# A linear-attention and bilinear feed-forward kernel: fewer and wider unread products, three weight pieces moved forward, one more tile in the planned stage

## The chip, the cores and the metric

The kernel runs on one core of one Trainium2 chip. A core has TensorE (PE in the profile; its weight loads are PEld), VectorE (DVE), ScalarE (ACT), GpSimd (POOL) and SyncE (SP), each with its own queue of instructions that it works off in order. SP mostly issues DMAs; ACT and POOL issue a few too. The metric is the device time of one execution in microseconds (us).

## What is computed

```python
# q, k, v, f_logit: (4, 8, 768, 48) float32
f = 1 / (1 + exp(-f_logit))
for t in range(768):
    state = f[:, :, t, :, None] * state + einsum('bhd,bhe->bhde', k[:, :, t], v[:, :, t])
    y[:, :, t] = einsum('bhd,bhde->bhe', q[:, :, t], state)
x = y.transpose(0, 2, 1, 3).reshape(3072, 384)
# w_a, w_b: (384, 1536), w_out: (1536, 384)
out = ((x @ w_a) * (x @ w_b)) @ w_out
```

The first part is a linear attention with a decay per channel, over 4 batches and 8 heads; the second a bilinear feed-forward block over 3072 tokens. The three weight matrices come as 64-bit floats and are turned into 32-bit ones on the chip, bit by bit[...].

## The kernel before

**Attention** is cut into 16 units: a batch, a half of its 768 positions (384, `BLK`) and four of its eight heads. A unit has fronts and a core. The front (`front_parts`, L296) makes the sigmoids of f on ACT (L306, L309), an affine step on POOL (L312), running products of f and of its inverse by scans on DVE (L316, L329), and multiplies k and q by them (L333). The core takes scores on PE (`scores`, L387), masks them on DVE (`mask`, L400), transposes k (`turn` on PE, L411; `turned`, its copy out on ACT), makes the gains of the state (`gains`, L435) and sums them (`carried`, L462 and L464), and adds the part within a chunk (`within`, L484) and the part that comes from the state (`across`, L510). ACT and DVE copy the result out of PSUM (`out_of_bank`, L529), and DMAs (`stored`, L549) bring it, transposed by its layout, into `xT`, a block of 384 tokens by 384 channels. Two units make a block; there are 8 blocks.

**Weights** come in 20 pieces (`weight_pieces`, L36): pieces 1 and 2 are the first 128 columns of w_b and w_a, then pairs of w_b and w_a for 256 columns each, then 128 columns again, then six pieces of w_out. `load_weights` issues the DMA of the next piece on SP into one of four raw buffers (pieces 5 and 6 have places of their own). `from_double` (L52) converts one in three parts: two ACT passes (L58, L59) and one POOL pass (L60); two more ACT passes (L62, L63); then DVE passes (L68, and L73, one for each of three row groups). `begin(n)` emits the first two parts up to piece n (`begin(8.5)` stops after the first part of piece 9), `end(n)` the third part, and after most pieces one more `load_weights`. A tile of the feed-forward part, `up(blk, ft)`, is 6 calls (12 matmul records, L593) for 128 columns of w_b and of w_a and one block; it needs `needed(ft)` pieces ended: tile 3 needs six, tiles 7 and 8 need ten. `product()` copies the w_b result of the oldest tile on ACT and multiplies it on DVE (L613, L615), which gives its two PSUM banks back; there are four such banks.

**Order.** The head of the kernel, up to the call of `up(0, 5)` and a little beyond (L965 to L1084), is an order written out by hand for all engines: units 0 to 3, the first weight pieces and tiles 0 to 5 of block 0. `keep_up(n)` (L954) emits n products of the identity with itself into a PSUM bank that nobody reads. Then a loop over `ups` (L1092) emits one tile after the other with the conversions between them; its length is `alone`. The remaining tiles of block 1 and everything after them form the list `main`: for blocks 2 to 7 a scheme with fewer multiplications for the first product (`up_triples`, its matmuls at L715), and for all blocks one for the second (`down`, matmuls at L808). A list scheduler (L1132 to L1274) walks through `main`; at every step its `fill` places work of the other lines (fronts, cores, loads, sums of weights, of w_out and of x) where its cost estimates find room by `BEAT`, the time of one call on PE. It knows the engines as free when it starts.

What the change and the steps below touch:

- `keep_up` at L953 to L957, called at L982, L988 and L1031, each time ahead of work that comes from other engines: `turn(0)`, `turn(1)` and `up(0, 0)`
- `end(6)` at L1060, `begin(8.5)` at L1079, `begin(9)` at L1083, with `up(0, 2)` to `up(0, 5)`, `across(3)` and `y_of(3)` (three ACT copies and five SP stores) around them
- `alone` at L1091
- `products_of_f[0]`, the running products of f of unit 0, which lie in `groups`

Of the kernel before, what the change touches and what calls it, by code (L numbers as in the profile page):

```python
# [22 lines left out]
BLK = 384  # L23
# [12 lines left out]
def weight_pieces(w_ba, w_out, moe_w_a, moe_w_b, moe_w_out, apart=1):  # L36


    w_b, w_a = (w_ba[:, i] for i in range(2))
    NKT, NFT, DM = w_ba.shape[2], w_out.shape[1], w_out.shape[2]  # L40
    for ft, n in [(0, 1)] + [(ft, 2) for ft in range(1, NFT - 1, 2)] + [(NFT - 1, 1)]:
        for dst, src in ((w_b, moe_w_b), (w_a, moe_w_a)):
            cols = slice(ft * 128, (ft + n) * 128)
            yield dst[:, :, cols], src.rearrange("(kt p) c -> p kt c", p=128)[:, :, cols], (NKT, n * 128)
    for ft in range(0, NFT, 2):
        rows = moe_w_out[ft * 128:(ft + 2) * 128]
        place = w_out.rearrange("p (j k) c -> p k j c", j=apart)
        to = place[:, ft // apart, ft % apart:ft % apart + 2] if apart > 1 else w_out[:, ft:ft + 2]
        yield to, rows.rearrange("(k p) c -> p k c", p=128), (2, DM)


def from_double(nc, dst, raw, k, h, bit, sgn, whole, apart=False):  # L52

    words = raw.bitcast(U32).rearrange("p k (n two) -> p (k n) two", two=2)
    lo, hi = words[:, :, 0], words[:, :, 1]
    width = lo.shape[1]
    h, bit, sgn = (x[:, 0:width] for x in (h, bit, sgn))
    nc.scalar.activation(h, hi.bitcast(FP32), AF.Abs, scale=HI_SCALE)  # L58
    nc.scalar.activation(bit.bitcast(FP32), lo, AF.Identity, bias=whole, scale=2.0**-29)  # L59
    nc.gpsimd.tensor_scalar(h, h, HI_MAX, None, ALU.min)  # L60
    yield
    nc.scalar.activation(sgn, hi.bitcast(FP32), AF.Sign)  # L62
    nc.scalar.activation(  # L63
        bit.bitcast(U16).rearrange("p (n two) -> p n two", two=2)[:, :, 1], sgn, AF.Relu, scale=-32768.0
    )
    yield
    hu = h.bitcast(U32)
    nc.vector.tensor_scalar(hu, hu, 3, None, ALU.logical_shift_left)  # L68
    hu, bit = (x.rearrange("p (k n) -> p k n", k=k) for x in (hu, bit))
    dst = dst.bitcast(U32)  # L70

    for rows in ([slice(i, i + 1) for i in range(k)] if apart else [slice(0, k)]):
        nc.vector.tensor_tensor(dst[:, rows], hu[:, rows], bit[:, rows], ALU.add)  # L73
    yield
# [62 lines left out]
def by_quotients(ctx, tc, q, k, f_logit, v, moe_w_a, moe_w_b, moe_w_out, out, ident, weights, bad):  # L137
    nc = tc.nc
# [60 lines left out]
    def load_unit(u, names="fkqv"):  # L199
        for do in loads_of(u, names):  # L200
            do()
# [34 lines left out]
    todo, raws, going = list(weight_pieces(w_ba, w_out, moe_w_a, moe_w_b, moe_w_out, NFT // 3)), [], []  # L236
    begun, ended = [0], [0]

    def load_weights(n=1):
        for _ in range(n):  # L240
            if len(raws) == len(todo):
                return
            dst, src, (k, m) = todo[len(raws)]
            raw = dst
            if src.dtype != FP32:

                if len(raws) in EARLY:
                    raw = groups[:, EARLY.index(len(raws))].bitcast(mybir.dt.uint64)
                else:
                    raw = next(raw_places)  # L250
                raw = raw[:, 0:k * m].rearrange("p (k m) -> p k m", k=k)
            nc.sync.dma_start(out=raw, in_=src)
            raws.append(raw)

    def begin(n):

        while 2 * n > begun[0] < 2 * len(todo):
            i, second = divmod(begun[0], 2)
            dst, src, shape = todo[i]
            if not second:  # L260
                going.append(
                    from_double(
                        nc, dst, raws[i], shape[0], next(blocks), bits[i % len(bits)], sign, whole, shape[0] == NKT
                    )
                    if src.dtype != FP32 else iter(())
                )
            next(going[i], None)
            begun[0] += 1

    def end(n):  # L270

        while ended[0] < min(n, len(todo)):
            begin(ended[0] + 1)
            next(going[ended[0]], None)
            ended[0] += 1
            if ended[0] > 2 and ended[0] - 1 not in EARLY:
                load_weights()
# [12 lines left out]
    products_of_f = {u: firsts[:, u] if u in FIRST else sets[u % NSET]["f"] for u in range(NU)}  # L290
# [60 lines left out]
    ps_f = [ps_a.tile([128, 512], FP32, tag=f"ps_f{i}", name=f"ps_f{i}") for i in range(4)]  # L351
    idle = list(range(4))
# [50 lines left out]
    def turn(u):  # L403

        kf = halves(sets[u % NSET]["k"])
        live.setdefault(u, {})["kT"] = sb1.tile([128, 2, NC, 128], FP32, tag="kT", name="kT")
        ps = live[u]["turned"] = [ps_f[idle.pop(0)] for _ in range(2)] if u in FIRST else pair_of(away(u))
        for n in range(2):
            for c in range(NC):
                o = n * BLK + c * C  # L410
                nc.tensor.transpose(ps[n][:, c * C:c * C + C], kf[:, o:o + C], ident)  # L411
# [10 lines left out]
    def gains(u, chunks=range(NC)):  # L422

        _, half, _ = unit(u)
        t, kT = sets[u % NSET], live[u]["kT"]
        last = half == NH - 1
        ps = live[u]["turned"]
        for n in range(2):
            for c in chunks:
                for p in range(2):  # L430
                    if last and c == NC - 1 and p == 1:
                        continue
                    for h in range(2):
                        r = slice(SUB * p, SUB * p + SUB)
                        nc.tensor.matmul(  # L435
                            ps[p][R * h:R * h + D, (n * NC + c) * D:(n * NC + c) * D + D],
                            lhsT=kT[r, n, c, R * h:R * h + D],
                            rhs=t["v"][r, n, c, h * D:h * D + D],
                            start=True,
                            stop=True,  # L440
                        )
        if chunks[0]:
            return
        st = sb3.tile([128, NJ, 2, D], FP32, tag="st", name="st")
        before = live[u - NQ]["st"][NJ] if half else None
        live[u]["st"] = [before] + [st[:, j] for j in range(NJ - 1 if last else NJ)]
# [46 lines left out]
    def across(u):  # L493

        b, half, qd = unit(u)
        qf, st, ps = halves(sets[u % NSET]["q"]), live[u]["st"], live[u]["y"]

        order = [(n, c, o, p) for n, c, o in each() for p in range(2)]
        if u in FIRST:

            order = sorted(order[::-1], key=lambda x: -x[3])
        elif half:
            order = [(n, c, o, p) for n, c, o in reversed(list(each())) for p in range(2)]
        for n, c, o, p in order:
            j = 2 * c + p
            if j == half == 0:
                continue
            for h in range(2):
                r, e = slice(R * h, R * h + D), R * (p ^ h)
                nc.tensor.matmul(  # L510
                    ps[p][e:e + D, o:o + SUB],
                    lhsT=st[j][r, n],
                    rhs=qf[r, tokens(n, c, p)],
                    start=False,
                    stop=True,
                    skip_group_check=True,
                )
# [63 lines left out]
    def up(blk, ft):  # L581

        for _, _, _, do, *args in up_steps(blk, ft):
            do(*args)
# [353 lines left out]
    with tc.manual_schedule():  # L938
# [14 lines left out]

        def keep_up(n):  # L954

            for _ in range(n):
                nc.tensor.matmul(ps_f[idle[-1]][:, 0:128], lhsT=ident, rhs=ident, start=True, stop=True)  # L957

        def y_of(u):
            for part in range(3):  # L960
                out_of_bank(u, part)
            stored(u)
# [16 lines left out]
        for _ in range(3):  # L979
            next(fronts[0])  # L980
        begin(1)
        keep_up(9)  # L982
        turn(0)
        turned(0)
        scores(0)
        begin(2)
        gains(0)
        keep_up(12)  # L988
        for _ in range(3):
            next(fronts[1])  # L990
        turn(1)
# [36 lines left out]
        load_weights()  # L1028
        load_unit(3, "k")
        load_unit(3, "q")  # L1030
        keep_up(30)  # L1031
        up(0, 0)
        emit_all(others[1])
        begin(4)
# [20 lines left out]
        begin(6.5)  # L1055
        up(0, 2)
        across(2)
        end(5)
        next(fronts[3])
        end(6)  # L1060
        y_of(2)
        load_weights(2)
        product()
# [12 lines left out]
        end(8)  # L1076
        carried(3)
        product()
        begin(8.5)  # L1079
        up(0, 5)  # L1080
        across(3)
        y_of(3)
        begin(9)  # L1083
        product()  # L1084


# [1 line left out]
        for i in range(8, NFT):  # L1088
            ups += [(1, i - 8), (0, i)]
        ups += [(1, i) for i in range(NFT - 8, NFT)]  # L1090
        alone = len(todo) - 6  # L1091
        for n, (blk, i) in enumerate(ups[0:alone]):  # L1092
            convert(needed(i))
            up(blk, i)
# [528 lines left out]
```

## Time and profile before

| | |
|---|---|
| three runs | 604.84, 607.16, 608.56 us, median 607.16 |
| the profiled execution | 606.54 us, of which the span of the instructions is 604.70 |
| busy: PE, DVE, ACT, POOL | 577.5, 411.9, 268.7, 76.3 us |
| mean granted TensorE clock | 0.991 |
| largest idle times of PE after the first 30 us | 2.44 (before 76.61), 1.13 (before 56.09), 0.93 (before 260.08), 0.62 (before 85.40), 0.62 (before 146.28) |

By stage, busy time of PE, DVE and ACT in us:

| stretch, us | what runs | PE | DVE | ACT |
|---|---|---|---|---|
| 0 to 34 | units 0 and 1, first weights | 21.42 | 25.46 | 18.70 |
| 34 to 86 | tiles 0 to 7 of block 0, units 2 and 3 | 47.81 | 34.34 | 42.41 |
| 86 to 128 | tiles one by one, weights | 42.00 | 19.57 | 31.13 |
| 128 to 196 | planned: last tiles of block 1, first `down` | 67.32 | 60.47 | 22.09 |
| 196 to 310 | planned: blocks 2 and 3 | 111.08 | 92.14 | 54.79 |
| 310 to 605 | planned: the rest | 287.91 | 179.96 | 99.61 |

A row of the timeline gives the start, the time that a run of like instructions takes, the engine, the line, the operation, what it writes and reads, their number, and in brackets the idle time of that engine before it with what ended that. A call of `matmul` on 32-bit floats shows as two records.

### The profile page before, as it was taken

To read this page: it belongs to the slowest core of one execution; us is meant where nothing else is said; L and a number is where in the kernel's file an instruction comes from. 1 tells how busy PE (TensorE), PEld (TensorE's weight loads), DVE (VectorE), ACT (ScalarE), POOL (GpSimd) and SP (SyncE) were. 2 spreads that over 40 slices of the span, in tenths; PEclk is the share of its full clock that TensorE was granted. 3 is DMA by queue.
4 is the path that set the end of the run, shared out by engine and by line. 5 is a ranking of instruction groups with operands and counts; after the bars stand their busy time and mean duration, and the time that the engine had idled before them with its cause. 6 is when DMAs were issued, how large, how long until landed. Compare 5 with 4: busy or idle time off the path is not lost.

```text
span 604.7 us, 14106 instructions
## 1 busy us (share of the span) xinstructions
PE 577.5 (96%) x5880; PEld 521.3 (86%) x5880; DVE 411.9 (68%) x786; ACT 268.7 (44%) x507; POOL 76.3 (13%) x71
## 2 busy tenths in 40 slices
PE   3899989999999999999999999999999999999995
PEld 3785545556999999989989999999999999999995
DVE  6889344568988768968895768846775165745741
ACT  5578588853321546325531353326331335134300
POOL 6254144435200000000000000000000000000000
PEclk9799999999999999999999999999999999999998
DMA  8685579239945134044003420032001100000000
GB/s 214 174 249 174 193 219 294 68 54 171 174 113 135 37 80 98 4 119 105 2 2 83 114 55 2 1 86 60 2 1 48 47 0 1 2 26 1 1 29 31
DMA packets 33273, 49.44 MB, mean 82 GB/s; under 512 B 3952, under 2 KB 24976, under 8 KB 33200
## 3 DMA queue, kind: packets, MB, share of 16 engines
q1 hardware_dynamic: 30000, 42.38, 25.7%
q0 software_dynamic: 3056, 5.92, 5.7%
q8 instruction: 48, 0.79, 0.6%
q14 instruction: 25, 0.20, 0.1%
q10 hardware_dynamic: 144, 0.15, 0.1%
HBM read 33.23 MB, written 4.72 MB: 63 GB/s over the span
## 4 chain that ended last, share of the span: by engine, by line
PE 80%; DVE 11%; ACT 4%; issue 3%; DMA 1%; SPq 0%; DVEq 0%; ACTq 0%
PE ps_f L715 33%; PE ps_f L808 26%; PE ps_f L593 12%; PE ps_y L484 2%; DVE groups L707 2%; PE ps_x L387 2%; PE ps_y L510 2%; DVE sums L707 1%; DVE inv L329 1%; PE ps_x L435 1%; PE ps_f L957 1%; PE ps_x L411 1%; DVE f_in L316 1%; DVE st L464 1%; DVE spare L329 1%
## 5 line engine op out<-in xcount | busy, mean ns | idle before, releaser
L593 PE MATMUL ps_f<-xT,w_ba 128*128 128x384 f32 x288 | 96.0, 490 | 4.2 <-DVE w_ba L73 3.6
L1271 ACT COPY sums<-ps_f 128x384 f32<-128x384 f32 x120 | 57.5, 480 | 85.1 <-PE ps_f L715 75.7
L593 PEld LDWEIGHTS ps_f<-xT,w_ba 128*128 128x128 f32 x288 | 53.6, 190 | 41.8 <-ACT spare L59 3.0
L1271 ACT COPY groups<-ps_f 128x384 f32<-128x384 f32 x120 | 57.7, 481 | 59.6 <-PE ps_f L715 39.3
L715 PE MATMUL ps_f<-xT,w_ba 128*128 128x192 f32 x384 | 78.2, 326 | 0.0
L715 PEld LDWEIGHTS ps_f<-xT,w_ba 128*128 128x128 f32 x384 | 64.7, 190 | 0.1
L715 PE MATMUL ps_f<-x_sums,raw 128*128 128x192 f32 x288 | 53.7, 330 | 1.9 <-DVE groups L707 1.3
L715 PE MATMUL ps_f<-groups,w_ba 128*128 128x192 f32 x288 | 55.5, 328 | 0.0
L808 PE MATMUL ps_f<-w_out,groups 128*128 128x192 f32 x288 | 51.8, 329 | 0.6 <-ACT x_sums L613 0.6
L808 PE MATMUL ps_f<-w_out,sums 128*128 128x192 f32 x288 | 51.9, 328 | 0.0
L715 PEld LDWEIGHTS ps_f<-x_sums,raw 128*128 128x128 f32 x288 | 47.0, 190 | 5.0 <-DVE groups L707 2.9
L808 PE MATMUL ps_f<-spare,sums 128*128 128x192 f32 x288 | 49.5, 327 | 0.0
L808 PEld LDWEIGHTS ps_f<-w_out,groups 128*128 128x128 f32 x288 | 47.1, 190 | 1.6 <-ACT x_sums L613 1.2
L715 PEld LDWEIGHTS ps_f<-groups,w_ba 128*128 128x128 f32 x288 | 47.9, 190 | 0.4 <-ACT groups L1271 0.2
L808 PEld LDWEIGHTS ps_f<-w_out,sums 128*128 128x128 f32 x288 | 47.2, 190 | 0.4
L808 PEld LDWEIGHTS ps_f<-spare,sums 128*128 128x128 f32 x288 | 47.1, 190 | 0.1
L312 POOL TENSOR_SCALAR inv<-inv 128x768 f32<-128x768 f32 x14 | 13.1, 935 | 267.4 <-ACT inv L309 267.3
L60 POOL TENSOR_SCALAR sums<-sums 128x768 f32<-128x768 f32 (+1 forms) x20 | 39.1, 1954 | 51.7 <-ACT sums L58 47.1
L707 DVE TENSOR_TENSOR sums<-sums,groups 128x768 f32<-128x768 f32 x36 | 34.9, 970 | 14.3 <-ACT groups L1271 13.9
L707 DVE TENSOR_TENSOR sums<-ps_f,sums 128x384 f32<-128x384 f32 x60 | 32.8, 552 | 15.6 <-PE ps_f L715 14.3
L715 PE MATMUL ps_f<-xT,raw 128*128 128x192 f32 x192 | 39.6, 329 | 0.5 <-ACT sums L1271 0.5
L715 PE MATMUL ps_f<-x_sums,w_ba 128*128 128x192 f32 x192 | 39.2, 327 | 0.0
(136 smaller groups left out, 883.4 us busy)
## 6 DMA issues: line engine op xcount, KB each, us to landing
raw<-w_ba POOLq DMA_DIRECT2D x11, 512.0 KB, 7.8
k_in<-in_k_dram SPq DMA_DIRECT2D x32, 144.0 KB, 4.4
q_in<-in_q_dram SPq DMA_DIRECT2D x32, 144.0 KB, 4.7
v_in<-in_v_dram SPq DMA_DIRECT2D x16, 288.0 KB, 5.2
raw<-in_moe_w_out_dram SPq DMA_DIRECT2D x6, 768.0 KB, 5.7
out_dram<-o SPq DMA_DIRECT2D x24, 192.0 KB, 1.9
f_in<-in_f_logit_dram SPq DMA_DIRECT2D x28, 144.0 KB, 3.0
xT<-y SPq DMA_DIRECT2D x45, 72.0 KB, 2.1
```

What stands on the lines that cost most here:

```text
L60: nc.gpsimd.tensor_scalar(h, h, HI_MAX, None, ALU.min)
L312: nc.gpsimd.tensor_scalar(inv, inv, EXP_K, 1.0, ALU.mult, ALU.add)
L316: nc.vector.tensor_tensor_scan(F[:, c], F[:, c], none, math.exp(MIDDLE), ALU.mult, ALU.add)
L329: nc.vector.tensor_tensor_scan(inv[:, w], inv[:, w], none[:, 0:C], first, ALU.mult, ALU.add)
L387: nc.tensor.matmul(ps[h][SUB * p:SUB * p + SUB, o:o + SUB], lhsT=kf[r, tokens(n, c, p)], rhs=qf[r, tokens(n, c, p)], start=True, stop=True,)
L484: nc.tensor.matmul(ps[p][e:e + D, o:o + SUB], lhsT=t["v"][r, n, c, h * D:h * D + D], rhs=at[r, h, o:o + SUB], start=o == 0, stop=True, ski ...
L510: nc.tensor.matmul(ps[p][e:e + D, o:o + SUB], lhsT=st[j][r, n], rhs=qf[r, tokens(n, c, p)], start=False, stop=True, skip_group_check=True,)
L593: nc.tensor.matmul(ps[nm][:, 0:BLK], lhsT=w[:, kt, ft * 128:ft * 128 + 128], rhs=xT[blk][:, kt], start=kt == 0, stop=kt == NKT - 1,)
L707: nc.vector.tensor_tensor(to, x, y, op)
L715: nc.tensor.matmul(ps[:, g], lhsT=sums_of_w[name][:, g, 128 * j:128 * j + 128], rhs=sums_of_x[blk][name], start=start and g == 0, stop=Tru ...
L808: nc.tensor.matmul(to, lhsT=x[:, i // 2, i % 2], rhs=w[:, NI * (i % 2) + i // 2], start=start and i == 0, stop=i == HFT - 1, skip_group_ch ...
L1271: do(*args)
```

## The change

Three things. `keep_up` multiplies the identity with the running products of f of unit 0 instead of with itself, 384 columns wide instead of 128, and is called for 2, 4 and 6 calls instead of 9, 12 and 30. In the order written by hand, the last conversion part of piece 6 stands ahead of the products of k and q of unit 3 (`next(fronts[3])`); and ahead of `up(0, 5)` stand the first two parts of pieces 9 and 10 and the last part of piece 9 (with the load of piece 13 that follows it), where the first part of piece 9 stood there alone, its second part after `y_of(3)`, and the rest in the loop. The loop makes 13 tiles instead of 14, so tile 7 of block 1 comes into the planned list.

```diff
         def keep_up(n):
 
+            x = products_of_f[0][:, 0]
             for _ in range(n):
-                nc.tensor.matmul(ps_f[idle[-1]][:, 0:128], lhsT=ident, rhs=ident, start=True, stop=True)
+                nc.tensor.matmul(ps_f[idle[-1]][:, 0:BLK], lhsT=ident, rhs=x, start=True, stop=True)
...
         begin(1)
-        keep_up(9)
+        keep_up(2)
         turn(0)
         turned(0)
         scores(0)
         begin(2)
         gains(0)
-        keep_up(12)
+        keep_up(4)
...
-        keep_up(30)
+        keep_up(6)
         up(0, 0)
...
         up(0, 2)
         across(2)
-        end(5)
+        end(6)
         next(fronts[3])
-        end(6)
         y_of(2)
...
         carried(3)
         product()
-        begin(8.5)
+        begin(10)
+        end(9)
         up(0, 5)
         across(3)
         y_of(3)
-        begin(9)
         product()
...
-        alone = len(todo) - 6
+        alone = len(todo) - 7
         for n, (blk, i) in enumerate(ups[0:alone]):
             convert(needed(i))
             up(blk, i)
```

## The prediction

> **What bounds the kernel now.** I read the page first, then the chain of waits, then PE's timeline for each idle stretch, and then the other engines there.
>
> ```profile
> PE 577.5 (96%) x5880; PEld 521.3 (86%) x5880; DVE 411.9 (68%) x786; ACT 268.7 (44%) x507; POOL 76.3 (13%) x71
> PE   3899989999999999999999999999999999999995
> PEclk9799999999999999999999999999999999999998
> ```
>
> TensorE is busy 577.5 of 604.7 us, and the chain puts 80% of the span on it. The change takes no arithmetic away from what is computed, so it can win only TensorE's idle time, time on unread products, and time at a reduced clock. Nearly all of that lies before 86 us. PE's timeline, with the idle time before a row in brackets:
>
> ```profile
> 29.61 7.54 PE L957 MATMUL ps_f<-ident 128*128 128x128 f32 x60
> 36.99 4.04 PE L593 MATMUL ps_f<-xT,w_ba 128*128 128x384 f32 x12
> 56.09 2.20 PE L593 MATMUL ps_f<-xT,w_ba 128*128 128x384 f32 x6 [1.13 <-DVE w_ba L73]
> 76.61 8.17 PE L593 MATMUL ps_f<-xT,w_ba 128*128 128x384 f32 x24 [2.44 <-DVE w_ba L73]
> 85.40 55.74 PE L593 MATMUL ps_f<-xT,w_ba 128*128 128x384 f32 x172 [0.62 <-ACT x_sums L613]
> ```
>
> There are four places: unread products right before the first tile of the feed-forward part, and three waits of 1.13, 2.44 and 0.62 us for converted weights or for a bank that an ACT copy empties. From 85.40 on the tiles follow each other without a gap.
>
> **Unread products.** One call is two matmul records. The 30 narrow ones at 29.61 take 7.54 us. A 128x384 record takes 4.04/12 = 0.33 us at full clock, so six wide calls are 12 x 0.33 = 4.0 us. They start at half clock, as now:
>
> ```profile
> 21.00:22.00 1.00, 0.22 (x16) 0.07 (x7) 0.93 (x4) 0.97 (x3) 0.58 (x1) 1.00 1.10 265
> 24.00:24.50 0.50, 0.33 (x12) 0.33 (x16) 0.50 (x4) 0.00 (x0) 0.50 (x1) 0.52 0.06 15
> 30.50:31.00 0.50, 0.50 (x5) 0.50 (x5) 0.47 (x2) 0.00 (x0) 0.00 (x0) 0.65 0.46 129
> 31.00:31.50 0.50, 0.50 (x7) 0.50 (x6) 0.50 (x1) 0.00 (x0) 0.24 (x1) 1.00 0.37 105
> ```
>
> (Columns: stretch, length, busy PE, PEld, DVE, ACT, POOL, granted clock, DMA share, GB/s.) The clock is half from about 24.0 to 30.8. From 29.61 to 30.83 two wide records pass at 0.65 us, the other ten take 3.3: the end is at about 34.2 instead of 37.1. The first tile then waits for its input, which DMAs bring:
>
> ```profile
> xT<-groups ACTq DMA_DIRECT2D x1, 48.0 KB, 3.3
> raw<-in_moe_w_a_dram SPq DMA_DIRECT2D x1, 768.0 KB, 6.7
> ```
>
> (Issue to landing, last column.) The last store of xT on ACT's queue is issued at 32.3 and lands at 35.6; the last of SP at 31.95 + 3.3 = 35.25. So the tile starts at about 35.5 instead of 36.99, 1.5 us sooner, with some 1.3 us of idle PE before it. Of the 3.5 us cut, 2.0 are hidden by the stores.
>
> The other two groups, 9 to 2 and 12 to 4 (1152 to 768 and 1536 to 1536 columns), I cost at nothing: they stand at 10.38 to 14.1 and 16.25 to 19.2, where DVE runs unbroken (scans L316 and L329, products L333) and what follows waits for DVE (transposes for k at 12.6 and 18.9, scores for q at 13.5 and 19.75). If that cover were gone, the sum of their changes is about 1.4 us the first time and 0.3 the second. The products now also wait for the scan whose result they read; it ends at 7.9, before the identity that they wait for anyway (10.38). POOL and SP are not touched there.
>
> *A rule against this.* The rows: PE busy 1.17 us of the 3.0 from 21 to 24 was followed by half clock, but the gap of 2.44 us before 76.61 was not (granted clock 1.00 in every 2 us there). The Trainium skill, "TensorE: Matmul & The Clock Gate", Part 1, says that a free-running window of about 3.4 us decides: a busy one opens the clock, an idle one halves it[...]. By the rule a gap of 1.3 us leaves the clock alone and costs 0; by the row of 21 to 24 a window 39% busy is enough for half clock, and a window with 1.3 us idle is 62% busy, so it lies nearer to the gap at 74 that did no harm. If it did, one window at half clock costs 3.4/2 = 1.7 us and eats the 1.5. For the first group the rule asks for 3.4 us of work; two wide calls at half clock are 4 x 0.65 = 2.6 us, then transposes. If the clock stays half one window longer, cold scores (1.5 instead of 0.9 us) and gains push the second transpose by some 0.7 us, hidden; two windows longer push it from 19 to 22.3 and mask(1) by 2 us. The other way, a clock that is not halved at 24 saves about 2 us of the small products until 29.6. I take 0, bounds -2 and +2.
>
> **Sixth piece.** Its DVE half stands behind two products of k and q:
>
> ```profile
> 53.19 0.95 DVE L333 TENSOR_TENSOR k_in<-k_in,spare 128x768 f32<-128x768 f32 x1
> 54.06 0.95 DVE L333 TENSOR_TENSOR q_in<-q_in,f_in 128x768 f32<-128x768 f32 x1
> 54.92 0.55 DVE L68 TENSOR_SCALAR sums<-sums 128x768 uint32<-128x768 uint32 x1
> ```
>
> Its ACT half ended at 50.05. Put ahead of them, its first row is ready 1.75 us sooner, at about 54.3, and tile (0,3) goes from its first to its second half at 54.96 without the wait of 1.13. The two products come 1.7 us later (k at 55.8, q at 56.7), but the transposes that need them follow the tile at 57.1: still covered. No DMA is issued by this step. The DVE chain before it also starts sooner: mask(2) waits 0.99 us for scores(2) at 42.63, and with the tile 1.5 us sooner DVE reaches it at 41.64, 1.0 us gained. PE on its own is then at tile (0,3) at 51.55 and DVE's first row of piece five at 51.5: together 58.29 becomes 55.65, **2.6 us** for these two edits.
>
> **Ninth and tenth piece.** ACT is the bound from 70 to 86:
>
> ```profile
> 63.17 1.00 ACT L59 ACTIVATE spare<-raw,whole 128x768 f32<-128x768 uint32 x1
> 70.19 1.46 ACT L529 COPY y<-ps_y 128x384 f32<-128x384 f32 x3 [6.02 <-PE ps_y L510]
> 71.68 0.90 ACT L62 ACTIVATE spare<-raw 128x768 bf16<-128x768 f32 x1
> 73.54 0.83 ACT L613 COPY x_sums<-ps_f 128x384 f32<-128x384 f32 x2
> 84.90 0.82 ACT L613 COPY x_sums<-ps_f 128x384 f32<-128x384 f32 x2
> ```
>
> ACT idles 6.02 us because y_of(3) waits for across(3), and then has everything to do at once. The change puts the second half of piece nine (0.90 + 1.06) and all of piece ten (3.6) into that hole: 5.6 us into 6.0. POOL's 2.2 us for piece ten moves with it (POOL is idle 9.74 us there), DVE's 2.2 us for piece nine fall into DVE's idle 6.88. On SP the load of piece thirteen (0.38 us) now stands ahead of the five stores of y_of(3); it waits for the raw buffer of piece nine, free about 65, long before the first store. Piece ten's load, issued at 57.64, lands 6.7 us later, at 64.3, just when ACT gets to it. Moved to the new times: pieces nine and ten on ACT 61.1 to 68.3, y_of(3) to 69.8 (PE's across(3) ends at 67.5), two copies, pieces eleven and twelve 70.7 to 77.8, the bank of tile (0,7) free at 78.8, needed at 79.6. Tile (0,7) finds its weights at 71.6, block 1's input lands at 74.2 and is needed at 75.7. So both waits go: **2.44 + 0.62 = 3.1 us**. If y_of(3) slips by more than 0.8 us, the bank is late and part of the 0.62 comes back.
>
> **One tile more in the list.** Planned work may start 3.9 us (one tile) sooner, before 128, where DVE is less than half busy:
>
> ```profile
> 128.00:196.00 68.00, 67.32 (x775) 58.55 (x774) 60.47 (x121) 22.09 (x39) 16.66 (x15) 1.00 0.74 142
> 196.00:310.00 114.00, 111.08 (x1422) 105.64 (x1421) 92.14 (x175) 54.79 (x115) 4.91 (x5) 1.00 0.25 61
> ```
>
> (Columns as above.) No work is added. The most to win is PE's idle time there, 0.68 + 2.92 = 3.6 us; the order of everything after is planned anew, and nothing excludes a loss of the same size. I take 0.5, near nothing, since DVE, 89% busy in the first row, gets some slack.
>
> **Sum** against the profiled execution (606.54, its span 604.70 and 1.84 around it): 2.6 + 3.1 + 0.5 = 6.2, so 600.3. The median of the three runs is 0.62 above that execution: **601.0**.
>
> **The rivals.**
> - *ACT or the stores stay the bound.* For it: the hole is filled to 0.4 us and piece ten's load lands just in time; the first tile waits for stores in any case. Against: in the shifted timeline every need has 0.8 us or more. If the keep-up gain is lost and half of the 3.1 returns, 1.1 + 1.5 + 0.5 = 3.1 us: 604.
> - *The list gets better.* If slack takes most of the 3.6 us: 598.
> - *The list gets worse.* One mechanism: twelve units of attention are interleaved after 128 us; if each meets the wait of 0.93 us that one meets at 260.08 (PE behind DVE's sum at L837), 12 x 1.0 = 12 us against 5.7: 613. It decides from 0.5 us per unit, where the gain is gone. For it: DVE at 89%. Against: PE loses only 3.6 us in 182 today, and the extra tile gives DVE room rather than work.
> - *The clock.* Fewer products than the clock needs: 5.7 + 0.5 - 2 = 4.2 us, 603; hardly more, since dense tiles follow.
>
> **How the numbers follow.** Main case 0.55 (599 to 603), better list 0.13, ACT or stores 0.13, clock 0.07, worse list 0.12. About 1% (6.1 us) is what a measurement of this kernel tells from no change; 601.0 lies on that bound, so a little over half of the main case counts as faster: 0.31 + 0.13 = 0.44. Within 1%: 0.24 + 0.13 + 0.07 = 0.44. Slower 0.12. The range, 597.5 to 606, leaves out the worse list and the far end of the better one.
>
> **What would show it.** Right: no idle of TensorE before the tiles at 54, 72 and 80 us, about 1.3 us idle before the first tile at 35.5, ACT busy from 61 to 70, tile (0,8) at 79.6 instead of 85.4, granted clock 1.00 from 31 on. Wrong: ACT waiting for piece ten's load, half clock after 34, more than 4 us of idle TensorE between 124 and 310.

## The result and the profile after

The changed kernel takes 597.96 us (median of 6 runs, 597.65 to 598.48) beside 606.08 for the kernel before: ratio 0.986, 95% interval 0.983 to 0.9889. In a later comparison it took 598.95 beside 605.44: 0.9884, 0.9865 to 0.9904. By the medians that is 8.1 and 6.5 us; 6.2 were forecast. The page after:

```profile
span 596.2 us, 13953 instructions
PE 571.8 (96%) x5802; PEld 512.0 (86%) x5802; DVE 412.3 (69%) x786; ACT 269.3 (45%) x507; POOL 77.0 (13%) x71
PEclk9999999999999999999999999999999999999998
```

The span is 8.5 us shorter, PE's busy time 5.7 us. The second slice (15 to 30 us) had a 7 in the old row of the clock, since half clock began in it; here it has a 9. PE's timeline at the places that the prediction named:

```profile
27.56 4.14 PE L958 MATMUL ps_f<-groups,ident 128*128 128x384 f32 x12
31.53 0.81 PE L593 MATMUL ps_f<-xT,w_ba 128*128 128x384 f32 x2
33.73 3.46 PE L593 MATMUL ps_f<-xT,w_ba 128*128 128x384 f32 x10 [1.39 <-DMA xT<-y]
...
48.67 1.16 PE L510 MATMUL ps_x<-q_in,st 48*48 48x64 f32 x48 [0.48 <-DVE st L464]
50.35 4.11 PE L593 MATMUL ps_f<-xT,w_ba 128*128 128x384 f32 x12 [0.52 <-DVE w_ba L73]
...
66.20 63.48 PE L593 MATMUL ps_f<-xT,w_ba 128*128 128x384 f32 x196
```

Read it against the old rows. The first tile ends 3.8 us sooner (33.73 + 3.46 = 37.19 against 41.03), and as forecast it now waits for the stores of its input (1.39 us, after its first two records). The wait of 1.13 inside tile (0,3) is gone, but two new ones of 0.48 and 0.52 stand before it. From tile (0,6) on, at 66.20, there is no gap up to 129.7: the waits of 2.44 and 0.62 have vanished, so tile (0,8) starts near 78.0 (three tiles of 3.9 us later) where it started at 85.40. Of the 8.5 us, 3.8 are there by tile (0,6), 7.4 by tile (0,8), and 1.1 come later. The stretch that was at half clock, first before and then after the change (columns: stretch, length, busy PE, PEld, DVE, ACT, POOL, granted clock, DMA share, GB/s):

```profile
24.00:31.00 7.00, 6.63 (x151) 6.27 (x152) 4.35 (x14) 1.90 (x4) 1.23 (x1) 0.51 0.06 17
24.00:31.00 7.00, 6.43 (x155) 4.88 (x156) 5.70 (x17) 1.90 (x4) 2.43 (x3) 1.00 0.15 43
```

The clock, the third number from the end, was 0.51 and is 1.00, and the small products before the tiles end 2 us sooner (27.56 against 29.61, the start of the third group of unread products). ACT, with its idle time in brackets:

```profile
66.36 1.46 ACT L529 COPY y<-ps_y 128x384 f32<-128x384 f32 x3 [0.21 <-PE ps_y L510]
75.92 0.83 ACT L613 COPY x_sums<-ps_f 128x384 f32<-128x384 f32 x2
```

The old hole of 6.02 us before y_of(3) is 0.21 us: piece ten ends at 66.15 (66.36 less the 0.21), and ACT is ready almost exactly when PE has finished across(3). The last row, the copy that frees the bank of tile (0,7), is 9 us sooner than at 84.90. What came after the loop, by stretches of 68 and 114 us like the old ones:

```profile
122.00:190.00 68.00, 66.89 (x861) 58.35 (x860) 58.61 (x120) 20.23 (x38) 14.00 (x13) 1.00 0.69 137
190.00:304.00 114.00, 112.65 (x1423) 107.22 (x1423) 92.98 (x177) 53.88 (x113) 3.34 (x4) 1.00 0.25 60
```

PE idles 1.11 + 1.35 = 2.46 us there, against 3.60.

### The profile page after: what moved, and what is told of

The parts are those of the page before. It is cut to its first block, busy times and chain, and to the rows that moved or that the text cites. A ratio compares the mean times of both kernels' runs of the same rounds, so it can differ in the third digit from the quotient of the medians.

```text
span 596.2 us, 13953 instructions
## 1 busy us (share of the span) xinstructions
PE 571.8 (96%) x5802; PEld 512.0 (86%) x5802; DVE 412.3 (69%) x786; ACT 269.3 (45%) x507; POOL 77.0 (13%) x71
## 4 chain that ended last, share of the span: by engine, by line
PE 84%; DVE 10%; issue 2%; ACT 1%; DMA 1%; SPq 0%; DVEq 0%; ACTq 0%
PE ps_f L715 35%; PE ps_f L808 28%; PE ps_f L593 13%; PE ps_y L484 2%; DVE inv L329 2%; PE ps_y L510 2%; PE ps_x L387 2%; PE ps_x L435 1%; PE ps_x L411 1%; DVE sums L707 1%; DVE groups L707 1%; DVE spare L329 1%; DVE f_in L316 1%; DVE q_in L333 1%; DVE w_ba L73 1%
```

## The experiments

Every kernel below was run five times or more beside the kernel before on the same chip. Ratios are to the kernel before. Only two of them (without the third group, and the new waits on DVE) ran beside the changed kernel, so most differences from it go from one comparison to another, and are given against both of its medians, 597.96 and 598.95.

**One part at a time.** The kernel with the old unread products and all else changed:

```diff
-            x = products_of_f[0][:, 0]
             for _ in range(n):
-                nc.tensor.matmul(ps_f[idle[-1]][:, 0:BLK], lhsT=ident, rhs=x, start=True, stop=True)
+                nc.tensor.matmul(ps_f[idle[-1]][:, 0:128], lhsT=ident, rhs=ident, start=True, stop=True)
...
-        keep_up(2)
+        keep_up(9)
...
-        keep_up(4)
+        keep_up(12)
...
-        keep_up(6)
+        keep_up(30)
```

> The changed kernel with the old unread products (9, 12 and 30 of 128 columns); pieces and list as changed. Theory A (the new products keep the clock at full between 24 and 31 us and are also shorter): this loses 4 us against the changed kernel, 602 us, 0.993 of before, and its profile shows half clock in some stretch between 20 and 31 us. Theory B (the full clock in the one profile was luck of the window's phase): it loses only the 1.5 to 2 us of shorter products, about 600 us, 0.989 of before.

599.86 us (598.33 to 603.38), 0.9918 (0.9892 to 0.9943): 0.9 to 1.9 us above the two medians of the changed kernel. That is the time of theory B. The spread, and the half clock in the profile, are what theory A expects. Its fastest run, with a mean granted clock of 0.999, took 598.33; runs at 0.991 took 600.13 and 601.09, one at 0.988 took 603.38. In its profile:

```profile
29.20 8.14 PE L957 MATMUL ps_f<-ident 128*128 128x128 f32 x60
37.18 4.04 PE L593 MATMUL ps_f<-xT,w_ba 128*128 128x384 f32 x12
...
25.00:31.00 6.00, 5.88 (x120) 5.52 (x113) 3.89 (x11) 1.91 (x4) 0.89 (x2) 0.50 0.07 20
```

Half clock from 25 to 31.7, and the 60 narrow records stretch to 8.14 us (7.54 in the old profile, where less of them fell under half clock).

The new unread products alone:

> The kernel before with the new unread products alone. Theory A: 4 us faster than before (0.993 to 0.994), full clock from 14 us on, the first tile near 33, but the waits of 2.4 us before 74 and of about 1 us before 54 stay. Theory B: 1.5 to 2 us faster (0.997). Rival (first tile is hidden by DVE later): under 1 us.

604.46 us, 0.999 (0.9977 to 1.0003): next to nothing, as the rival has it, although in the trace the first tile ends 4.1 us sooner than in the old profile.

```profile
53.29 2.20 PE L593 MATMUL ps_f<-xT,w_ba 128*128 128x384 f32 x6 [1.17 <-DVE w_ba L73]
73.83 21.61 PE L593 MATMUL ps_f<-xT,w_ba 128*128 128x384 f32 x61 [2.46 <-DVE w_ba L73]
...
74.00:78.00 4.00, 4.00 (x8) 2.16 (x8) 2.63 (x6) 3.94 (x6) 2.71 (x2) 0.59 0.45 140
```

The lead is 2.8 us at 53.29 and 73.83 (56.09 and 76.61 before), as PE meets two new waits for DVE on the way, of 0.38 and 0.47 us. But the old profile is of an execution with half clock. The kernel with the longer list alone (below) has the old order up to its list, and its profile has full clock here:

```profile
35.45 4.04 PE L593 MATMUL ps_f<-xT,w_ba 128*128 128x384 f32 x12
...
68.50 4.14 PE L593 MATMUL ps_f<-xT,w_ba 128*128 128x384 f32 x12
75.10 8.17 PE L593 MATMUL ps_f<-xT,w_ba 128*128 128x384 f32 x24 [2.46 <-DVE w_ba L73]
83.87 51.87 PE L593 MATMUL ps_f<-xT,w_ba 128*128 128x384 f32 x160 [0.61 <-ACT x_sums L613]
```

Beside this one the first tile ends 2.5 us sooner (36.95 against 39.49), and of that 1.3 us are left at 73.83 (against 75.10). The wait of 2.46 us, still there, was followed in this execution by about 3.4 us of half clock (0.59, the third number from the end, in the stretch from 74 to 78, where 8 instead of some 12 records ran). At half speed that costs some 1.7 us, an estimate from the 3.4, so it takes the lead back. The fastest of the 11 runs, 603.42 us, is 1.4 below the 604.79 of the kernel before at a clock of 0.995 or more (median of the 34 such runs in all comparisons), as the lead of 1.3 would have it. How many of the other runs lost the lead to half clock after that wait is not shown.

Pieces nine and ten alone:

> The kernel before with pieces 9 and 10 moved alone. If ACT's hole was what cost the two waits of 2.44 and 0.62: 3.1 to 3.6 us faster, 0.994 to 0.995 of before, tiles from (0,6) on without a gap. Rival (ACT or the stores of block 1 stay the bound without the gain at the first tile): 1 us or less.

603.51 us, 0.9959 (0.994 to 0.9978), 2.5 us faster. Its runs fall into two groups again: three at a clock of 0.995 or more took 601.50 to 601.86, nine at 0.992 or less 602.69 to 605.03. The trace has no wait left from tile (0,6), at 71.79, to the end of the loop:

```profile
71.79 67.35 PE L593 MATMUL ps_f<-xT,w_ba 128*128 128x384 f32 x208
```

So the rival that ACT or the stores stay the bound falls; at like clock the gain is the 3.1 us of the sum (the three runs have a median of 601.68, against 604.79).

The longer list alone:

```diff
-        alone = len(todo) - 6
+        alone = len(todo) - 7
```

> The kernel before with 13 tiles in the loop alone. From the two traces (idle TensorE after the loop 3.6 us before, 2.5 after): 1.1 us faster, 0.998. Rival (the new plan is better or worse by luck): anywhere within 3 us, with the idle time of TensorE after 124 us telling which.

603.87 us, 0.9989 (0.9975 to 1.0004). Seven runs at 0.996 or more took 603.35 to 603.93, about 1.1 us below the 604.79. In the two stretches after the loop:

```profile
126.50:194.50 68.00, 67.44 (x860) 58.11 (x858) 59.09 (x119) 20.26 (x38) 15.31 (x14) 1.00 0.70 141
194.50:308.50 114.00, 112.65 (x1353) 107.22 (x1355) 92.93 (x176) 53.53 (x113) 3.35 (x4) 1.00 0.25 61
```

PE idles 1.91 us instead of 3.60. The interval of the ratio includes 1, so that there is a gain at all rests on the trace (1.7 us less idle time) and on the runs at like clock (1.1).

**Piece six, from the other side.** The changed kernel with that move undone:

```diff
-        end(6)
+        end(5)
         next(fronts[3])
+        end(6)
```

> The changed kernel with the last part of piece 6 back behind the products of k and q of unit 3. If the move is worth the wait that it removes: TensorE waits about 1.2 us before the second half of tile (0,3), near 53 us, and the time is 0.6 to 1.1 us above the changed kernel (598.6 to 599.1). Rival (ACT is late by then anyway): same time, 598.

599.90 us (599.48 to 600.88), 0.9898 (0.987 to 0.9926), 0.95 and 1.94 above the two medians of the changed kernel, where 0.6 to 1.1 were expected. The old wait is back inside tile (0,3):

```profile
54.13 2.20 PE L593 MATMUL ps_f<-xT,w_ba 128*128 128x384 f32 x6 [1.17 <-DVE w_ba L73]
```

**One more tile in the list.** The changed kernel with `alone = len(todo) - 8` and the last conversions emitted before the list:

> The changed kernel with 12 tiles in the loop instead of 13 (all conversions emitted before the list begins). If room for DVE ahead of the list is what pays: the idle time of TensorE after 122 us falls from 2.5 to 2 us or less, 597.5 us. Rival (the gain was the luck of one plan, or the last conversions now stand in the way of the list): 598 to 600 us.

601.29 us, 0.9911 (0.9882 to 0.9941), 2.3 to 3.3 us slower than the changed kernel, and worse than both forecasts. The plan now puts scores where DVE has not finished q. PE waits where it had not, and half clock follows (granted clock 0.50 from 129 to 132 us; in the second row, with columns as above, the mean is 0.97):

```profile
128.57 1.48 PE L387 MATMUL ps_x<-q_in,k_in 48*64 48x64 f32 x48 [1.82 <-DVE q_in L333]
122.80:190.80 68.00, 64.92 (x840) 55.86 (x839) 57.56 (x117) 17.54 (x36) 13.56 (x12) 0.97 0.64 128
```

Its idle time after the loop is 4.15 us against 2.46, and about 3.4 us at half clock cost some 1.7 more, an estimate from their length. PE is ready for these scores at 126.75 (128.57 less the wait), 3.0 us sooner than in the changed kernel (129.73), but DVE has q ready only 1.2 us sooner (128.52 against 129.68); on DVE the last conversion, from 114.44 to 116.16, stands right before the list. So one tile more gave a better plan, and two, with all conversions ahead of the list, a worse one. How much of the loss comes from the conversions was not tried alone.

**What the unread products do.** First, narrow products with as many columns as the new wide ones (the identity with itself, 6, 12 and 18 calls of 128 columns):

> The changed kernel with narrow products of the identity with itself, as many columns as the wide ones (6, 12 and 18 calls of 128). Theory A (wide products themselves keep the clock up): a third or more of the runs lose one or two windows at half clock (mean granted clock 0.992 or less), median 599 us or more. Theory B (they only have to be short, so that tiles follow sooner): 598 us, all runs within 1 us, as the changed kernel.

599.15 us (598.18 to 599.41), 0.9879 (0.9851 to 0.9906). Three of six runs have a clock of 0.991 or 0.992, as theory A says, but they took 599.33 to 599.41, only 1.2 us more than the one at 0.997. Its profile has half clock from 25 to 31.7 and yet

```profile
30.23 4.98 PE L957 MATMUL ps_f<-ident 128*128 128x128 f32 x36
35.05 4.34 PE L593 MATMUL ps_f<-xT,w_ba 128*128 128x384 f32 x12
```

the tile starts 2.1 us sooner than behind the 60 records above. The median lies between those of the old products (599.86) and of the changed kernel, so a part of the gain needs no width, only fewer records ahead of the tile.

No unread products at all, and only the third group dropped:

> The changed kernel without any unread product. If the clock needs them: TensorE is idle for 6 us before the first tile, which starts at half clock; 2 to 4 us slower than the changed kernel (600 to 602), mean granted clock 0.993 or less in all runs. Rival (they are not needed, since stores and DVE set the time of the first tiles): within 0.5 us of the changed kernel.

> The changed kernel without the third group of unread products (the first two kept). The first tile then begins when its input lands[...]. If half clock at the first tile is hidden by DVE and ACT behind it: 598 to 598.5 us. If the third group is what keeps the start of the tiles fast: 600 us or more.

598.49 us (597.47 to 598.91), 0.9868 (0.984 to 0.9896), and 599.47 us (598.60 to 599.90), 0.9895 (0.9878 to 0.9912). The first did not lose the 2 to 4 us that "the clock needs them" expects: it is 0.5 above the one median of the changed kernel and 0.5 below the other. The second lies between its two forecasts. Without any, the first tile waits 4.82 us and then takes 6.87 us at half clock:

```profile
32.55 6.87 PE L593 MATMUL ps_f<-xT,w_ba 128*128 128x384 f32 x12 [4.82 <-DMA xT<-y]
```

It ends 2.2 us later than in the changed kernel, and tile (0,6) starts 0.8 us later (67.03 against 66.20). In between, the two waits for DVE of 0.48 and 0.52 us that the changed kernel has do not occur, since TensorE is later: 1.4 of the 2.2 us are made up there. Without the third group alone, half clock lasts from 29.9 to 40.1, all six runs have a clock of 0.989 or 0.990, and the cost is 0.5 us beside the changed kernel in the same comparison, 1.5 beside the first one.

The third group alone, without the first two:

> The changed kernel with the third group of unread products alone (the first two dropped). If the first two only keep TensorE warm under work that waits for DVE: within 0.7 us of the changed kernel (598 to 599), although the scores of units 0 and 1 run at half clock (1.5 us instead of 0.9). Rival (the cold products of units 0 and 1 reach the masks on DVE late): 600 us or more, with DVE waiting for TensorE between 19 and 25 us.

597.26 us (597.08 to 598.60), 0.9866 (0.984 to 0.9891): the lowest median of all, though its interval overlaps that of the changed kernel. The scores of units 0 and 1 run at half clock (1.56 us each), and DVE does not notice: its two masks start at 19.74 and 23.25, against 19.67 and 23.16 before the change.

```profile
20.00:22.00 2.00, 2.00 (x66) 1.73 (x68) 1.80 (x6) 1.81 (x5) 0.14 (x1) 0.50 1.08 362
```

**The changed kernel again, and the new waits on DVE.**

> The changed kernel once more, for the spread of its runs. If the wide products hold the clock: mean granted clock 0.993 or more in nearly all runs and all times within 1 us of 598. If the six runs so far were luck: some runs at 0.992 or less, and if half clock costs little here all the same, those are within 1 us of the others too.

598.95 us (596.96 to 599.25), clock 0.994 to 0.999: the clock is as "the wide products hold it" expects, the times spread a little more. With the first comparison that makes 12 runs, median 598.30, none at 0.992 or less.

The last kernel moves the small products of `hand_on` of units 0 and 1 to GpSimd (cut at the dots):

```diff
-            nc.vector.tensor_scalar(before[:, n], ...)
+            eng = nc.gpsimd if u in FIRST else nc.vector
+            eng.tensor_scalar(before[:, n], ...)
```

> The changed kernel with hand_on of units 0 and 1 (four small products, 1.12 us of DVE ahead of the first product) on GpSimd. If DVE sets the time between 40 and 54 us: the two waits of 0.48 and 0.52 us before across(2) and tile (0,3) go and the time falls by 0.7 to 1.0 us, 597.1. Rival (ACT, which is behind only 0.2 us there, takes the gain back before tile (0,8)): 597.8.

598.21 us (598.11 to 599.54), 0.9885 (0.9865 to 0.9905): no gain that can be told from the changed kernel (598.95 in the same comparison, 597.96 in the first). The wait of 0.48 is gone, the one before tile (0,3) stays:

```profile
50.53 4.11 PE L594 MATMUL ps_f<-xT,w_ba 128*128 128x384 f32 x12 [0.55 <-DVE w_ba L73]
```

In this execution half clock lasted from 24.3 to 27.7, and the first tile goes on at 34.71, 1 us later than in the profile after; the second profile of the changed kernel has 34.75 without half clock. So this trace does not decide whether ACT takes the gain back.

## Why the prediction came out as it did

The direction and the range were right, and the steps mostly carried. The 597.96 lies near the low end of the range, where the prediction had put "the list gets better" (598), but not for that reason: the list gave about 1.1 us, not most of the 3.6. The term that moved was the clock.

- *Pieces nine and ten, 3.1 us.* Shown: 3.1 at like clock with this part alone, the waits of 2.44 and 0.62 gone, ACT's hole filled to 0.21 us in the changed kernel. From the start of tile (0,6) to that of (0,8) the traces give 3.6.
- *Piece six and the first tile, 2.6 us together.* Undoing piece six costs 0.95 to 1.94, undoing the unread products 0.9 to 1.9. At full clock on both sides tile (0,6) starts at 68.50 in the old order, and at 66.20 and 66.87 in the two profiles of the changed kernel: 1.6 to 2.3 us. The two do not stand alone: by the ratio the new products alone are worth 0.6 us. Their lead at the wait of 2.46 us is 1.3 at full clock, and in the one trace half clock after that wait took it back. With the wait gone, they pay.
- *The first two groups, at nothing.* Borne out: with both dropped the time is 597.26, and the masks on DVE are within 0.1 us of where they were.
- *One tile more, 0.5 us.* Too small: 1.1 by the runs at like clock. The bounds of 3.6 to both sides were fair, since the next step in the same direction lost 2.3 to 3.3.
- *The clock, 0 with 2 to both sides.* This term was mis-sized, and it is the one behind the surplus of the first comparison, at the far end that the prediction had named (about 2 us for small products at full clock). The sum was made against an execution with half clock from 24.0 to 30.8, taken over unchanged: the first tile was to start at 35.5, and it came at 31.5 (two records) and 33.7 (the rest), because the small products and the third group ran at full clock, and with them the stores were issued sooner. In 60 later runs of the kernel before, 34 have a clock of 0.995 or more (median 604.79) and 24 of 0.992 or less (median 606.90): over 2 us that come and go by run, in the number that the sum starts from. That the forecast was made from an execution of the slower kind is chance, and so is the mix in the first comparison (by their times, three of the six runs before are of each kind). At like clock the gain is 604.79 - 598.30 = 6.5 us, near the sum of 6.2. The changed kernel lost the clock less often in its runs (none of 12 at 0.992 or less, against 24 of 60); but the longer list alone, with the old products, had only two of 12 there, so the share differs from one comparison to another. That a loss can cost less is shown by the narrow products and by the kernels without some of them. Whether the width of the products by itself holds the clock is open: narrow ones of the same columns had three of six runs at 0.992 or less, which points that way, but with the wide ones the changed kernel without piece six had one in six, and the new products alone three in 11.
- *The gap of 1.3 us before the first tile harms no clock.* Borne out: 1.39, and full clock after; so too after 1.57 in its second profile. The row that was read as harmless, the wait of 2.44 us at 74, was not always so: with the new products alone the same wait was followed by half clock. The rule that the prediction set against its rows would have left the clock alone there; the measurement decides. The move of pieces nine and ten removed that risk too, which the prediction did not count.
- *The worse list* did not come with one tile. It came with two, by the mechanism named (PE behind DVE), but in one place, with 1.82 us and half clock after it.

## What to carry to other kernels

Products that nobody reads, put in to hold the clock, stand in TensorE's queue: cut them to what fits into the wait, and test dropping each group, since here none at all cost 0.5 us at most, and the third group alone did as well as all three. Cutting them pays only where no wait behind them takes the time back. Work that an engine could do while it waits for another belongs ahead of the waiting instruction in its queue; look for the longest idle time in front of a burst. When a profile has a stretch at half clock, compare runs at like granted clock before a sum starts from it.

## What was not expected of the hardware

A partly idle stretch was followed by half clock in some executions and not in others with nearly the same work: after PE had been busy 1.17 of 3.0 us (21 to 24) in the old profile it was, in the profile after with 1.12 us in the same stretch it was not; a wait of about 2.45 us was followed by it once in the three profiles that have it (the new products alone), and the wait of 1.82 us with two tiles more was followed by it too. Half clock then lasted about 3.4 us (74.7 to 78.1 in the first of these), 6.8 (24.0 to 30.8 in the old profile) or, where TensorE was idle at its beginning, 10.2 (29.9 to 40.1 without the third group). And at the start of an execution the granted clock reads 1.00 while the same 48 score matmuls take 1.56 us instead of 0.93 (without the third group, at 14.66): the row is not yet the clock.
